# Reordering the products of the first pair, its loads and the staging sums of a gated feed-forward kernel

## The chip, the cores and the metric

The kernel runs on one NeuronCore of a Trainium2 chip. The metric is the device time of one execution, in microseconds (us). Each comparison was run on one chip with the kernel before beside it. All executions told of here were classed as fast ones. With a single core there is no second core to compare with, so a run counts as slow only where it is over 1.5% above the fastest of its kernel. Where a "slow execution" is spoken of below, one of about 542 us or more inside that class is meant.

Ratios are computed as the mean time of one kernel's fast runs over the mean of the other's fast runs of the same rounds, with a 95% interval. They are not quite the ratio of the medians that stand beside them.

## The reference

```python
B, S, D, F = 1, 2048, 1024, 3584           # all bfloat16
def reference(x, w_gate, w_up, w_down):
    return (gelu(x @ w_gate) * (x @ w_up)) @ w_down   # tanh approximation
```

## The kernel before

x is handled in two halves of 1024 rows (`h`), each as two column blocks of 512 (`xT[0]`, `xT[1]`, transposed, so that the contraction lies on the partitions). The 28 blocks of 128 columns of w_gate and w_up are taken two at a time: a **pair**. For a pair and for each of gate and up (`j`), the four products of two weight blocks with two x blocks are made with seven products instead of eight, by Strassen's method in Winograd's form. It needs sums of weight blocks (`s1` to `s4`, made by GpSimd, for the first pairs partly by VectorE) and sums of x blocks (`t1` to `t4`, made once by VectorE). The first two blocks of the first half (`first_units` and the loop over `k0`) are done in the classical way, in two halves of the contraction, since x arrives late at the start (the last of its block 1 landed at 18.50 us). The loads at the start:

```python
    for kd in range(KH, KD):
        load_xT(xT, 0, 0, kd, kd + 1)          # x block 0, second half, by DMA transposes
        if kd == KH + 1:
            for j in range(2):
                load_w(first, j, 5, KD, act, 0, FA)   # rows 5..7 of w_gate, w_up, columns 0..255
    for j in range(2):
        load_w(first, j, 0, KD, sp, FA, FG)    # columns 256..511, all rows, 512 KB each
    for k0 in range(0, KD, KH):
        load_xT(xT, 0, 1, k0, k0 + KH)         # x block 1 in two halves
```

`act` and `sp` are the queues of ScalarE and SyncE, `KD` is 8 and `KH` is 4. Every operation goes through a helper that keeps the program order of its engine. `banks` are the eight PSUM banks, the buffers in which TensorE's products are collected; a bank has to be emptied before the next product goes there. `m5` is one of the seven products, which VectorE adds to others. One pair:

```python
        def m2():
            for j in range(2):
                mm(P_[j], j, block(key, j, 0, 1), b21, False)
                if j == 0:
                    g[0] = gelu(banks[P_[0]], nxt is None)
                else:
                    mult(hT, g[0], banks[P_[1]], f0, 0)       # VectorE, frees the PSUM bank
        ...
        if part != 1:
            for j in range(2):
                mm(P_[j], j, block(key, j, 0, 0), b11, True)  # product 1
                act(nc.scalar.copy(out=banks[QB[j]][:], in_=banks[P_[j]][:]))
        if part == 0:
            m2()
            return
        behind = len(pending) > 0
        if behind:
            pending.pop()()                                   # product 2 of the pair before
        done("m2 of last")                                    # hook: work for other engines
        ...
        for j in range(2):
            add_m5(QB[j], QB[j])                              # L412: VectorE adds m5 in PSUM
            prep(j, "s2")
        ...
```

and the order of the first pair:

```python
            first_units(hT)
            first_pair = PPG - 1                   # pair 1
            for j in range(2):
                s_sum(0, first_pair, j, "s1")
                s_sum(0, first_pair, j, "s3")
            s_sum(0, first_pair, 0, "s2", True)    # True: on VectorE
            s_sum(0, first_pair, 0, "s4", True)
            t_sum("t1")
            pair_quads(hT, 0, first_pair, (0, PPG), {}, 0)    # products 1 and 2
            ...
            t_sum("t2")
            for k0 in range(0, KD, KH):            # both classical halves
                ...
```

The second projection, by w_down, uses sums of w_down's blocks too. They are **staged** during the pairs of the first half: `stage_load(i)` brings two blocks of w_down, `stage_step(n)` makes one of three sums of them on VectorE (the first and the third into a new buffer, named `o_sb`, the second in place) and stores two of them to memory. There are 4 staging sums per pair. `stage_x` transposes columns of the next x in the same way, its first eight into place and its last eight into an `o_sb` buffer, from which `store_x` stores them. There are four `o_sb` buffers for both.

```python
    def stage_step(n):
        i, k = n // 3, n % 3
        w = staged[i][0]
        if k != 1:
            staged[i].append(o_pool.tile([P, DN], F32R, name="o_sb")[:])
        t = staged[i][-1]
        in0, in1 = (lambda: (w[:, 0, DN:D], w[:, 0, 0:DN]), ...)[k]()   # (cut)
        dve(nc.vector.tensor_tensor(out=t, in0=in0, in1=in1, op=ALU.subtract))
        if k > 0:
            sp(nc.sync.dma_start(out=t_dram[:, k - 1, i, :], in_=t.bitcast(F32)))
    ...
            if h == 0 and pair >= PPG:             # from pair 2 on
                n = [min(4 * (pair - PPG + d), NSTEP) for d in range(3)]
                steps = [lambda k=k: stage_step(k) for k in range(n[0], n[1])]
                new = range((n[1] + 2) // 3, (n[2] + 2) // 3)
                then["m2 of last"] = (
                    then.get("m2 of last", [])     # in even pairs: load 2 MB of weights
                    + steps[:2]                    # two sums at the pair's start ("early")
                    + [lambda q=q: stage_x(*q) for q in xs[:2]]
                )
                then["m7"] = [store_x] + [lambda i=i: stage_load(i) for i in new]
                then["m4"] = steps[2:]             # two at its end ("late")
                xs = xs[2:]
```

## Time and profile before

| | before |
|---|---|
| time, median of 3 runs | 541.68 us (541.52 to 541.92) |
| span of the profiled execution | 539.7 us |
| TensorE (PE) busy | 534.5 us, 99% |
| VectorE (DVE), ScalarE (ACT), GpSimd (POOL) busy | 67%, 49%, 44% |

One place it did not read is VectorE's timeline at the end of pair 2, 45 us. Columns: start, duration, engine, line, operation, output and inputs, shape, count, and in brackets the idle time with its releaser.

```profile
45.73 0.68 DVE L599 TENSOR_TENSOR o_sb<-wd_sb,o_sb 128x512 fp32r<-128x512 bf16 x1
46.33 1.64 DVE L599 TENSOR_TENSOR o_sb<-wd_sb 128x512 fp32r<-128x512 bf16 x1
```

L599 is the staging sum (L605 in the changed kernel). Where it doesn't have to wait for GpSimd it takes 0.68 us; 1.64 is what one takes that starts inside a GpSimd sum (here one from 45.79 to 47.43). The reader is to keep these two sizes in mind.

### The profile page before, as it was taken

Reading aid. Unit: us, or ns where it says so; the run is one execution under the profiler, and the core shown is the slowest. Engines: PE = TensorE matmul, PEld = TensorE weight load, DVE = VectorE, ACT = ScalarE, POOL = GpSimd, SP = SyncE. Lnnn points to the kernel's source line nnn. Section 1 sums busy time; section 2 is a strip of 40 time slices with the busy share of each in tenths; the row PEclk is TensorE's granted clock in tenths of the full one; section 3 lists DMA queues with packets and bytes.
Section 4 is the critical chain, followed back from the end, with each engine's and each line's share of the span. In section 5 each row is a group of like instructions: output and inputs, shape, how many; then the busy total and the mean of one; then the engine's idle time right before and its main releaser. Section 6 shows DMA issues by size and latency. Waiting matters only on the chain.

```text
span 539.7 us, 7117 instructions
## 1 busy us (share of the span) xinstructions
PE 534.5 (99%) x2384; PEld 377.1 (70%) x2384; DVE 362.2 (67%) x475; ACT 263.3 (49%) x446; POOL 239.5 (44%) x210
## 2 busy tenths in 40 slices
PE   8999999999999999999999999999999999999997
PEld 3577777666776676767776677777777766866865
DVE  0978777787875997889574434444444469969951
ACT  1555555555555319216465555555555551452270
POOL 1369877777776000000056776666777730000000
PEclk9999999999999999999999999999999999999999
DMA  9927687695827876789950404041331466677846
GB/s 231 310 84 215 203 247 227 198 274 185 286 77 252 296 244 223 257 265 314 319 187 1 156 1 157 9 147 55 102 110 48 157 199 218 229 242 242 288 147 209
DMA packets 84772, 102.70 MB, mean 190 GB/s; under 512 B 18688, under 2 KB 66304, under 8 KB 84736
## 3 DMA queue, kind: packets, MB, share of 16 engines
q1 hardware_dynamic: 61936, 80.30, 46.2%
q10 hardware_dynamic: 22800, 21.96, 13.2%
q8 instruction: 19, 0.31, 0.2%
q14 instruction: 17, 0.14, 0.1%
HBM read 85.98 MB, written 12.58 MB: 183 GB/s over the span
## 4 chain that ended last, share of the span: by engine, by line
PE 93%; SPq 2%; DVE 1%; issue 1%; DMA 1%; ACT 0%; ACTq 0%; DVEq 0%
PE bank L389 61%; PE bank L664 33%; SPq L172 2%; DMA xT<-in_x_dram 1%; SPq L161 0%; DVE hT L277 0%; DVE t_mem L245 0%; DVE bank L412 0%; DVE s_mem L358 0%; DVE t_mem L239 0%; ACT o_sb L717 0%; SPq L167 0%; ACTq L717 0%; DVEq L239 0%
## 5 line engine op out<-in xcount | busy, mean ns | idle before, releaser
L389 PE MATMUL bank<-t_mem,s_mem 128*128 128x512 f32 x1056 | 249.7, 394 | 0.2 <-DVE bank L412 0.2
L389 PEld LDWEIGHTS bank<-t_mem,s_mem 128*128 128x128 f32 x1056 | 198.2, 188 | 44.3 <-DVE bank L412 0.9
L360 POOL TENSOR_TENSOR s_mem<-w_mem 128x512 fp32r<-128x512 bf16 x104 | 121.9, 1195 | 196.8 <-DVE t_mem L245 116.2
L277 DVE TENSOR_TENSOR hT<-w_mem,bank 128x512 bf16<-128x512 f32 x104 | 71.2, 686 | 86.6 <-PE bank L389 46.2
L664 PE MATMUL bank<-t_mem,s_mem 128*128 128x512 f32 x544 | 127.2, 392 | 0.0
L664 PEld LDWEIGHTS bank<-t_mem,s_mem 128*128 128x128 f32 x544 | 102.1, 188 | 22.2
L412 DVE TENSOR_TENSOR bank<-bank,m 128x512 f32<-128x512 f32 x108 | 69.8, 693 | 44.9 <-ACT m L434 42.7
L389 PE MATMUL bank<-xT,w_mem 128*128 128x512 bf16 x432 | 98.1, 380 | 0.2 <-DMA w_mem<-in_w_up_dram 0.2
L272 ACT ACTIVATE w_mem<-bank 128x512 f32<-128x512 f32 x104 | 61.8, 596 | 54.0 <-DVE bank L412 36.3
L389 PEld LDWEIGHTS <-w_mem 128*128 128x128 bf16 x432 | 40.1, 98 | 52.1 <-issue 6.8
L574 DVE TENSOR_TENSOR t_mem<-w_mem 128x1024 fp32r<-128x1024 bf16 x56 | 65.6, 1217 | 0.0
L360 POOL TENSOR_TENSOR s_mem<-w_mem,s_mem 128x512 fp32r<-128x512 bf16 x50 | 62.2, 1268 | 0.0
L360 POOL TENSOR_TENSOR s_mem<-s_mem,w_mem 128x512 fp32r<-128x512 f32 x50 | 58.0, 1180 | 0.0
L439 ACT COPY bank<-bank 128x512 f32<-128x512 f32 x54 | 30.8, 570 | 39.0 <-PE bank L389 38.5
L373 ACT CAST s_mem<-w_mem 128x512 fp32r<-128x512 bf16 x54 | 33.0, 615 | 30.5 <-PE bank L389 29.2
L639 DVE TENSOR_TENSOR s_mem<-hT 128x512 fp32r<-128x512 bf16 x52 | 34.2, 685 | 10.2 <-PE bank L664 9.4
L434 ACT COPY m<-bank 128x512 f32<-128x512 f32 x54 | 31.7, 587 | 18.4 <-PE bank L389 18.3
L664 PEld LDWEIGHTS <-hT 128*128 128x128 bf16 x224 | 21.2, 98 | 26.7 <-issue 2.1
L444 ACT COPY bank<-bank 128x512 f32<-128x512 f32 x54 | 30.8, 570 | 12.8 <-PE bank L389 12.8
L717 ACT CAST o_sb<-bank 128x512 bf16<-128x512 f32 x28 | 15.3, 585 | 39.6 <-PE bank L664 39.6
L599 DVE TENSOR_TENSOR o_sb<-wd_sb,o_sb 128x512 fp32r<-128x512 bf16 x28 | 31.4, 1121 | 0.5
L571 ACT CAST t_mem<-w_mem 128x1024 fp32r<-128x1024 bf16 x28 | 26.9, 1047 | 0.0
(44 smaller groups left out, 235.7 us busy)
## 6 DMA issues: line engine op xcount, KB each, us to landing
t_mem<-t_dram SPq DMA_DIRECT2D x56, 512.0 KB, 5.4
w_mem<-in_w_gate_dram ACTq DMA_DIRECT2D x10, 1024.0 KB, 5.6
w_mem<-in_w_up_dram ACTq DMA_DIRECT2D x10, 1024.0 KB, 8.7
wd_sb<-in_w_down_dram SPq DMA_DIRECT2D x28, 256.0 KB, 5.0
t_dram<-o_sb SPq DMA_DIRECT2D x28, 256.0 KB, 2.4
wd_sb<-in_w_down_dram SPq DMA_DIRECT2D x12, 512.0 KB, 8.4
w_mem<-in_w_down_dram SPq DMA_DIRECT2D x10, 512.0 KB, 5.8
w_mem<-in_w_down_dram SPq DMA_DIRECT2D x4, 1024.0 KB, 6.3
```

Source lines behind the costliest of these rows:

```text
L272: act(nc.scalar.activation(out=g_sb, in_=ps[:], func=ACT.Gelu_apprx_tanh))
L277: nc.vector.tensor_tensor(out=hT[:, fc, tb * TB : (tb + 1) * TB], in0=g_sb, in1=ps[:], op=ALU.mult,)
L360: pool(nc.gpsimd.tensor_tensor(out=t, in0=in0, in1=in1, op=op))
L373: act(nc.scalar.copy(out=t, in_=a(1, 1)))
L389: nc.tensor.matmul(banks[bank][:], lhsT=lhs[:, c, :], rhs=rhs[:, c, :], start=start and c == 0, stop=c == KH - 1, skip_group_check=True,)
L412: nc.vector.tensor_tensor(out=banks[dst][:], in0=banks[src][:], in1=m5[j][:], op=ALU.add)
L434: act(nc.scalar.copy(out=m5[j][:], in_=banks[V_[j]][:]))
L439: act(nc.scalar.copy(out=banks[RB[j]][:], in_=banks[QB[j]][:]))
L574: dve(nc.vector.tensor_tensor(out=t, in0=in0, in1=in1, op=ALU.subtract))
L599: dve(nc.vector.tensor_tensor(out=t, in0=in0, in1=in1, op=ALU.subtract))
L639: dve(nc.vector.tensor_tensor(out=t, in0=in0, in1=in1, op=op))
L664: nc.tensor.matmul(banks[bset[u]][:], lhsT=lhs(i, u), rhs=rhs(i), start=start and i == 0, stop=stop and i == NS - 1, skip_group_check=True,)
```

## The change

Its intent: w_up's last rows take the other queue, so that ScalarE is not blocked; columns 256 to 511 and x's block 1 arrive in halves, each half of the weights ahead of the half of x that needs it; and the first pair follows that order: product 1, the first classical half, product 2 (`part` 2), the second classical half, the rest. VectorE's sums follow, s1 among them, which GpSimd made before; its multiply of product 2 (`out11`) is deferred, and the second half of t4 is split into two quarters between the additions of m5. Last, the staging sums run two steps late, so that pair 2 starts without any.

```diff
--- before.py
+++ after.py
@@ -208,10 +208,10 @@
         load_xT(xT, 0, 0, kd, kd + 1)
         if kd == KH + 1:
             for j in range(2):
-                load_w(first, j, 5, KD, act, 0, FA)
-    for j in range(2):
-        load_w(first, j, 0, KD, sp, FA, FG)
+                load_w(first, j, 5, KD, (act, sp)[j], 0, FA)
     for k0 in range(0, KD, KH):
+        for j in range(2):
+            load_w(first, j, k0, k0 + KH, sp, FA, FG)
         load_xT(xT, 0, 1, k0, k0 + KH)
     new_chunk((0, 1))
     for j in range(2):
@@ -425,8 +425,11 @@
                 mm(P_[j], j, block(key, j, 0, 1), b21, False)
                 if j == 0:
                     g[0] = gelu(banks[P_[0]], nxt is None)
-                else:
-                    mult(hT, g[0], banks[P_[1]], f0, 0)
+                elif part != 2:
+                    out11()
+
+        def out11():
+            mult(hT, g[0], banks[P_[1]], f0, 0)
 
         def do_m5(j):
             mm(V_[j], j, s(j, "s1"), tsum["t1"], True)
@@ -438,13 +441,14 @@
             mm(QB[j], j, s(j, "s2"), tsum["t2"], False)
             act(nc.scalar.copy(out=banks[RB[j]][:], in_=banks[QB[j]][:]))
 
-        if part != 1:
+        if part not in (1, 2):
             for j in range(2):
                 mm(P_[j], j, block(key, j, 0, 0), b11, True)
                 act(nc.scalar.copy(out=banks[QB[j]][:], in_=banks[P_[j]][:]))
-        if part == 0:
+        if part == 2:
             m2()
-            return
+        if part in (0, 2):
+            return out11
         behind = len(pending) > 0
         if behind:
 
@@ -467,11 +471,13 @@
                 done("m6")
         for j in range(2):
             add_m5(QB[j], QB[j])
+            done(f"q{j}")
             prep(j, "s2")
         done("m5")
         for j in range(2):
             mm(RB[j], j, s(j, "s3"), tsum["t3"], False)
             add_m5(V_[j], RB[j])
+            done(f"v{j}")
             prep(j, "s3")
             if j == 0:
                 g[1] = gelu(banks[V_[0]], nxt is None)
@@ -817,18 +823,15 @@
             first_units(hT)
             first_pair = PPG - 1
 
+            nxt = (0, PPG)
             for j in range(2):
-                s_sum(0, first_pair, j, "s1")
                 s_sum(0, first_pair, j, "s3")
-            s_sum(0, first_pair, 0, "s2", True)
-            s_sum(0, first_pair, 0, "s4", True)
+            pair_quads(hT, 0, first_pair, nxt, {}, 0)
             t_sum("t1")
-            pair_quads(hT, 0, first_pair, (0, PPG), {}, 0)
             for j in range(2):
                 s_sum(0, first_pair, j, "a22")
-            t_sum("b22")
-            s_sum(0, first_pair, 1, "s2", True)
-            t_sum("t2")
+                for name in ("s1", "s2"):
+                    s_sum(0, first_pair, j, name, True)
             for k0 in range(0, KD, KH):
                 for u, bset in enumerate((PB, RB)):
                     for b, w_sb in zip(bset, chunks[first]):
@@ -838,12 +841,16 @@
                         unit_out(hT, bset, u, 1)
                     if k0 > 0 and u == 0:
                         t_sum("t3")
+                if k0 == 0:
+                    out11 = pair_quads(hT, 0, first_pair, nxt, {}, 2)
+                    t_sum("b22")
+                    t_sum("t2")
+                    s_sum(0, first_pair, 0, "s4", True)
+            t_sum("t4", 0, KH // 2)
             s_sum(0, first_pair, 1, "s4", True)
-            t_sum("t4", 0, KH // 2)
             xs = [(tb, kd) for tb in (1, 0) for kd in range(KD)]
             new_x(1)
             stage_load(0)
-            stage_load(1)
         for pair in range(first_pair, NPAIR):
             then = {}
             if pair % PPG == 0 and (pair // PPG + 1) * PPG < NPAIR:
@@ -858,17 +865,20 @@
                     then["m2 of last"] = [load_chunk]
             if h == 0 and pair >= PPG:
 
-                n = [min(4 * (pair - PPG + d), NSTEP) for d in range(3)]
+                n = [
+                    min(max(4 * (pair - PPG + d) - 2, 0), NSTEP) for d in range(3)
+                ]
                 steps = [lambda k=k: stage_step(k) for k in range(n[0], n[1])]
+                early_steps = steps[: len(steps) - 2]
                 new = range((n[1] + 2) // 3, (n[2] + 2) // 3)
 
                 then["m2 of last"] = (
                     then.get("m2 of last", [])
-                    + steps[:2]
+                    + early_steps
                     + [lambda q=q: stage_x(*q) for q in xs[:2]]
                 )
                 then["m7"] = [store_x] + [lambda i=i: stage_load(i) for i in new]
-                then["m4"] = steps[2:]
+                then["m4"] = steps[len(early_steps) :]
                 xs = xs[2:]
             if pair == NPAIR - 2:
 
@@ -912,8 +922,8 @@
                 }
             if pair < PPG and h == 0:
 
-                def late_t4():
-                    t_sum("t4", KH // 2, KH)
+                def late_t4(c):
+                    t_sum("t4", c, c + 1)
                     last_on["t4"] = last_on["dve"]
 
                 def late_s():
@@ -922,7 +932,12 @@
                         for j in range(2):
                             s_sum(0, PPG, j, name)
 
-                then = {"m5": [late_t4], "m4": [late_s]}
+                then = {
+                    "q0": [lambda: late_t4(KH - 2)],
+                    "v0": [lambda: late_t4(KH - 1)],
+                    "v1": [out11],
+                    "m4": [late_s],
+                }
             nxt = (h, pair + 1) if pair + 1 < NPAIR else None
             part = 1 if (h, pair) == (0, PPG - 1) else None
             pair_quads(hT, h, pair, nxt, then, part)
```

## The prediction

> **What bounds the kernel now.** I read the page's table of engines first: TensorE (PE) is busy 534.5 of 539.7 us, while VectorE (DVE) has 67%, ScalarE 49%, GpSimd 44%. Part 4 of the page, the chain that ended last, is 93% PE. So only idle time or lost pitch of PE can be won, and a busy share does not show lost pitch, since one matmul's record (380 to 394 ns) is longer than the distance between two. I therefore read the timeline of PE over the first 50 us and divided distances between starts by counts. Columns: start, duration from first start to last end, engine, line, operation, tiles, shape, count, and in brackets the idle time with its releaser.
>
> ```profile
> 6.68 4.30 PE L253 MATMUL bank<-xT,w_mem 128*128 128x512 bf16 x18
> 11.13 2.33 PE L253 MATMUL bank<-xT,w_mem 128*128 128x512 bf16 x10 [0.15 <-DMA w_mem<-in_w_up_dram]
> 13.30 1.03 PE L389 MATMUL bank<-xT,w_mem 128*128 128x512 bf16 x4
> 14.54 2.76 PE L389 MATMUL bank<-xT,w_mem 128*128 128x512 bf16 x12 [0.21 <-DMA w_mem<-in_w_up_dram]
> 17.14 7.07 PE L253 MATMUL bank<-xT,w_mem 128*128 128x512 bf16 x32
> 23.86 7.78 PE L389 MATMUL bank<-t_mem,s_mem 128*128 128x512 f32 x32
> 31.85 2.10 PE L389 MATMUL bank<-t_mem,s_mem 128*128 128x512 f32 x8 [0.21 <-DVE bank L412]
> 33.80 1.90 PE L389 MATMUL bank<-xT,w_mem 128*128 128x512 bf16 x8
> 35.35 9.44 PE L389 MATMUL bank<-t_mem,s_mem 128*128 128x512 f32 x40
> 44.63 3.63 PE L389 MATMUL bank<-xT,w_mem 128*128 128x512 bf16 x16
> 47.91 2.42 PE L389 MATMUL bank<-t_mem,s_mem 128*128 128x512 f32 x9
> ```
>
> The steady part: from 14.54 to 17.14 twelve bf16 matmuls take 2.60 us, 0.216 each. From 35.35 to 47.91, 12.56 us, lie 40 f32 and 16 bf16 matmuls; less 16 x 0.216 = 3.46 that leaves 0.227 per f32 one. Later pairs repeat the same 12.56 us, so nothing is to be won after 33.8 us. Up to there: 6.68 to 11.13 is 4.45 us for 18 matmuls (3.89 needed): **0.56 lost**. 13.30 to 14.54 is 1.24 for 4 (0.86): **0.37 lost**. 17.14 to 31.85 is 14.71 for 32 bf16 and 32 f32 (6.91 + 7.26 = 14.17): **0.5 lost** (single starts put 0.11 at 29.5 and 0.37 just before 31.85). 31.85 to 33.80 is 1.95 for 8 (1.82): **0.1 lost**. In sum 1.5 us, all that this change can reach.
>
> What causes each: the ScalarE timeline tells of part of the first, the DVE timeline of the last two.
>
> ```profile
> 4.49 0.38 ACTq L161 DMA_DIRECT2D w_mem<-in_w_gate_dram  x1
> 7.46 0.47 ACTq L161 DMA_DIRECT2D w_mem<-in_w_up_dram  x1
> 8.03 0.58 ACT L314 COPY xT<-bank 128x512 bf16<-128x512 bf16 x1 [4.36 <-DMA w_mem<-in_w_gate_dram]
> ...
> ```
>
> ```profile
> 14.69 0.91 DVE L358 TENSOR_TENSOR s_mem<-s_mem,w_mem 128x512 fp32r<-128x512 f32 x1
> 15.63 1.52 DVE L358 TENSOR_TENSOR s_mem<-w_mem,s_mem 128x512 fp32r<-128x512 bf16 x1
> 17.07 3.24 DVE L236 TENSOR_TENSOR t_mem<-xT,xT 128x2048 fp32r<-128x2048 bf16 x1
> ...
> 28.78 1.28 DVE L412 TENSOR_TENSOR bank<-bank,m 128x512 f32<-128x512 f32 x2
> 29.98 1.21 DVE L245 TENSOR_TENSOR t_mem<-xT,t_mem 128x1024 fp32r<-128x1024 bf16 x1
> 31.11 1.28 DVE L412 TENSOR_TENSOR bank<-bank,m 128x512 f32<-128x512 f32 x2
> ```
>
> The tail of w_up (rows 5 to 7) is issued by ScalarE only at 7.46: its issue waits for an earlier load's semaphore, whose load landed at 7.44. ScalarE's copy of x block 3 stands behind it and ends at 8.61; PE's next weight load starts at 8.66, 0.25 us late. The same load lands at 11.09 and PE resumes at 11.13, 0.31 late. In the DVE timeline the engine has no gap from 14.69 to 32.4; the reader is to see that PE's third and fourth losses end on L412, the additions of m5, and that a 1.21 us half of t4 stands between the two pairs of them.
>
> **What the Trainium skill says.** "TensorE: Matmul & The Clock Gate", section "Wait — 56ns, not 53.3ns?", gives 215.7 ns between starts of warm 512-column matmuls; this trace agrees with 216 for bf16, and has 227 for the fp32r ones. "VectorE: DVE Perf Modes", "The perf-mode tier table", gives 2293 ns for an fp32 tensor_tensor of 2048 elements; t2 and t3 took 2.28 us here. "SBUF — State Buffer", "Who interferes with whom": a DVE instruction with two SBUF inputs contends with a GpSimd instruction that reads SBUF. The trace agrees: sums that take 0.68 us alone took 0.91 and 1.52, and t1 3.24 instead of 2.28, while GpSimd ran its four sums (12.78 to 18.16). "DMA: Bandwidth & Descriptors", "Issuing engines are not separate DMA queues": issuing from another engine saves only sequencer time. That fits a load whose harm was to block ScalarE's sequencer.
>
> **The change, part by part.** No matmul is added or removed; only the order and waits of the first 34 us change.
>
> 1. *w_up's tail moves from ScalarE's queue to SP's, between transposes.* SP can issue it about 4.9, or 5.7 at worst if it must await x's second load (landed 5.65), so it lands near 9.5 (estimate: 4.6 us from issue to landing for the 192 KB w_up load before it). PE wants it at 10.6. The copy no longer waits. Gain 0.25 + 0.31 = 0.56. Price: transposes of blocks 6 and 7 land some 0.6 us after their 9.47 and 9.95; PE wants them at 11.0 and 11.9, so hidden.
> 2. *Columns 256 to 511 load in k-halves.* Before, the two 512 KB loads landed at 12.71 and 14.49, and PE stopped until 14.54. Now both first halves together are 512 KB, so the second of them lands about when the first load did, 12.7. First units end at 13.30 - 0.56 = 12.74; product 1's second half wants it at 13.6. Gain 0.37.
> 3. *The classical half takes product 2's place.* It starts at 12.74 + 8 x 0.216 = 14.47 and needs the first half of transposed x, which landed at 16.51. With 512 KB less ahead of it, at the 1.8 to 2.0 us per 512 KB that the neighbouring landings show, it lands at 14.5 to 14.8. **New wait: 0.1 to 0.4.** Product 2 (from about 18.2) wants second halves at perhaps 16.7; the second classical half (from about 20.0) wants the other x half at 18.5 as before. Both hidden.
> 4. *DVE's order.* t1 starts at about 14.8 instead of 17.07, and GpSimd has only two sums left (s3), done by about 14.1, so t1 takes 2.28: done 17.1 instead of 20.3. It pays with two more s1 sums (2 x 0.60). By my walk in program order: four s-sums to 19.5, t2 to 21.8, s4 to 22.4, multiply 23.2, t3 25.5, multiply 26.1, half of t4 27.2, s4 27.8. Then the m5 additions and two t4 quarters of 0.6 interleave: additions done near 28.4, 29.6, 30.2, 31.4. PE, at about 23.4 when m5 starts, wants them at about 28.9, 29.8, 30.7, 31.6. All met, some by only 0.2. Gain 0.6 less about 0.1.
> 5. *Two staging sums leave the start of pair 2, the deferred multiply (0.65) enters.* DVE is freed of 2 x 0.7 to 0.8 where GpSimd makes pair 2's sums. Those were in time already (f32 block from 35.35 without a stall), so no gain on the path. Two sums appear later in pair 12, where DVE has a gap of 2.6 us: free.
>
> Sum: 0.56 + 0.37 + 0.6 = 1.5, less 0.25 for x's half and 0.1 for tight additions: 1.15 to 1.2 us. 541.68 - 1.2 = **540.5 us**.
>
> **Rivals.** (a) *x's first half becomes the new wait in full.* The transfer row shows those transposes slow (SP spent 5.40 us issuing the first); if they don't come earlier with fewer bytes ahead, PE waits from 14.5 to 16.5, and the kernel gets 0.5 to 1 us slower: about 542.4. Against it: the DMA engines are at their limit there (share about 1.1), so bytes, not issue, set the landing. (b) *DVE stays the bound.* Its work between 14.7 and 32 is nearly all there; if t1 gets no earlier start or the sums run beside GpSimd, items 1 to 3 are eaten by a wait on L412, and only 0.2 to 0.5 us remain: 541.3. For it: 17 us without a gap. Against: 1.0 us of t1's time was contention, and 2.3 us its late start. (c) *Everything hides*: all 1.5 gone, 540.1.
>
> **Range and chances.** The 2% mark is 10.8 us, seven times what is lost in the whole region, so faster by it is ruled out and slower would need a stall of a kind that nothing here suggests. Repeats of before spread 0.4 us. Range 539.9 to 541.3: low is (c) with spread, high is (b).
>
> **What would show it.** PE timeline of after: no gap on w_up near 11 or 14; 18 + 10 matmuls in about 6.05 us; a short wait on x's transpose near 14.5; no wait on L412; first pair over near 32.6 instead of 33.8; 12.56 us per pair afterwards. DVE: t1 in 2.28 us from about 14.8. The prediction is wrong if PE waits over 0.6 us for x's halves, if additions still end PE's waits, or if a later pair loses its pitch through the shifted staging sums.

## More of the kernel before

The page follows the chain of work that ended last back from the end; this is its share by engine:

```profile
PE 93%; SPq 2%; DVE 1%; issue 1%; DMA 1%; ACT 0%; ACTq 0%; DVEq 0%
```

Nearly everything that is not PE in it lies in the first 34 us. The prediction reads that region.

## The result, and the profile after

| | before, same rounds | after |
|---|---|---|
| median of 6 runs | 541.59 us | 542.61 us |
| lowest to highest | 541.22 to 541.92 | 540.65 to 544.28 |
| ratio of fast runs | | 1.0018 [0.9998, 1.0038] |

542.61 lies 1.3 us above the predicted range. The six times were 540.65, 542.7, 544.28, 542.36, 542.61 and 542.6. **The profile was taken of the first, which is the only one within the range.** So the profile after shows the kernel at its best, and nothing in it can show where the other five lost 2 us. Its chain:

```profile
PE 98%; DMA 1%; ACT 0%; issue 0%; DVE 0%; ACTq 0%
```

PE's timeline of the start, in the columns as before:

```profile
6.61 6.39 PE L253 MATMUL bank<-xT,w_mem 128*128 128x512 bf16 x28
12.84 1.89 PE L389 MATMUL bank<-xT,w_mem 128*128 128x512 bf16 x8
14.59 3.63 PE L253 MATMUL bank<-xT,w_mem 128*128 128x512 bf16 x16
18.05 1.89 PE L389 MATMUL bank<-xT,w_mem 128*128 128x512 bf16 x8
19.78 3.62 PE L253 MATMUL bank<-xT,w_mem 128*128 128x512 bf16 x16
23.04 9.46 PE L389 MATMUL bank<-t_mem,s_mem 128*128 128x512 f32 x40
32.35 1.90 PE L389 MATMUL bank<-xT,w_mem 128*128 128x512 bf16 x8
33.90 9.44 PE L389 MATMUL bank<-t_mem,s_mem 128*128 128x512 f32 x40
```

No line has a releaser. Product 1 (12.84), classical half (14.59), product 2 (18.05), half (19.78) and the forty fp32 matmuls follow one another at full pitch; 33.80 of before has become 32.35. VectorE's timeline, t1 and the end of pair 2:

```profile
14.63 2.29 DVE L236 TENSOR_TENSOR t_mem<-xT,xT 128x2048 fp32r<-128x2048 bf16 x1 [0.33 <-DMA xT<-in_x_dram]
...
44.28 1.58 DVE L605 TENSOR_TENSOR o_sb<-wd_sb 128x512 fp32r<-128x512 bf16 x1
45.89 1.53 DVE L605 TENSOR_TENSOR o_sb<-wd_sb,o_sb 128x512 fp32r<-128x512 bf16 x1
```

t1 takes 2.29 us instead of 3.24, as predicted. The two staging sums at 44.28 and 45.89 take one contended length each, and after them all is in time. From 33.90 on the pairs keep 12.56 us.

### The profile page after: what moved, and what is told of

Same layout as the page of the kernel before. It is cut to its first block, busy times and chain, and to the rows that moved or that the text cites. A ratio compares the mean times of both kernels' runs of the same rounds, so it can differ in the third digit from the quotient of the medians.

```text
span 538.9 us, 7121 instructions
## 1 busy us (share of the span) xinstructions
PE 533.7 (99%) x2384; PEld 377.3 (70%) x2384; DVE 363.8 (68%) x478; ACT 263.1 (49%) x446; POOL 236.5 (44%) x208
## 4 chain that ended last, share of the span: by engine, by line
PE 98%; DMA 1%; ACT 0%; issue 0%; DVE 0%; ACTq 0%
PE bank L389 63%; PE bank L670 33%; PE bank L253 3%; DMA w_mem<-in_x_dram 1%; PE bank L304 0%; ACT o_sb L723 0%; DVE xT L312 0%; ACTq L723 0%
## 5 line engine op out<-in xcount | busy, mean ns | idle before, releaser
L360 POOL TENSOR_TENSOR s_mem<-w_mem 128x512 fp32r<-128x512 bf16 x102 | 118.5, 1183 | 198.5 <-DMA w_mem<-in_w_up_dram 102.4
L277 DVE TENSOR_TENSOR hT<-w_mem,bank 128x512 bf16<-128x512 f32 x104 | 71.0, 686 | 82.9 <-PE bank L389 43.1
L412 DVE TENSOR_TENSOR bank<-bank,m 128x512 f32<-128x512 f32 x108 | 69.8, 694 | 46.5 <-ACT m L437 42.5
```

The costliest lines, as they stand in the source:

```text
L277: nc.vector.tensor_tensor(out=hT[:, fc, tb * TB : (tb + 1) * TB], in0=g_sb, in1=ps[:], op=ALU.mult,)
L360: pool(nc.gpsimd.tensor_tensor(out=t, in0=in0, in1=in1, op=op))
L412: nc.vector.tensor_tensor(out=banks[dst][:], in0=banks[src][:], in1=m5[j][:], op=ALU.add)
```

## The experiments

**Theory.** The reordered start gives its 1.2 us in all executions, and something later takes 2 us in most of them. The part of the change that reaches past 34 us is the staging schedule, so it is the first suspect. **Rival 1:** the slow executions lose the time at the start, where loads land a little differently each time. **Rival 2:** the six runs were a poor sample. Eighteen runs were made; the runs of one call shared a chip and the runs of the kernel before. This table has them all; the last column tells what TensorE lost after 34 us in the execution that was profiled (distance of two starts less the usual 0.227 us, if over 0.2 us in one place; in brackets what the first pair lost).

| run | median us (range), runs | before | ratio [95%] | profiled us: lost after 34 us |
|---|---|---|---|---|
| after_again | 543.06 (541.99 to 543.97), 6 | 541.67 | 1.0026 [1.0013, 1.004] | 541.99: 1.2 at 49, 0.3 at 128 |
| order_only | 540.8 (540.43 to 541.13), 5 | 541.67 | 0.9986 [0.9974, 0.9998] | 540.74: none |
| stage_only | 542.93 (542.01 to 544.74), 6 | 541.67 | 1.0029 [1.0015, 1.0043] | 542.93: 0.5 at 50, 0.9 at 54 |
| loads_only | 545.42 (545.24 to 546.1), 5 | 541.67 | 1.0075 [1.0062, 1.0087] | (start: 1.5, 1.5, 0.3, 0.6, 0.4) |
| moved_sums | 542.96 (542.45 to 544.25), 6 | 541.55 | 1.0023 [0.9994, 1.0051] | 542.82: 1.8 at 52 |
| early_sums | 541.32 (540.85 to 542.8), 6 | 541.55 | 0.9992 [0.9964, 1.0021] | 541.11: none |
| gpsimd_sums | 544.76 (543.75 to 545.6), 6 | 541.55 | 1.0046 [1.0015, 1.0077] | 545.6: 3.0 at 52, half clock after, 0.4 at 107 |
| old_loads | 542.3 (542.18 to 542.7), 4 | 541.55 | 1.0007 [0.9973, 1.004] | (start: 0.3, 0.4, 1.2) |
| after_third | 542.63 (542.43 to 542.78), 6 | 541.52 | 1.0015 [1.0003, 1.0028] | 542.7: 1.2 at 50, 0.2 at 104 |
| no_vector_sums | 540.87 (540.44 to 542.84), 6 | 541.52 | 0.9991 [0.9973, 1.0008] | 542.84: 1.6 at 102, 0.7 at 466 |
| late_start | 543.11 (542.11 to 546.43), 6 | 541.52 | 1.0035 [1.001, 1.006] | 546.43: 2.7 at 104, half clock after |
| order_again | 540.64 (540.35 to 542.81), 6 | 541.52 | 0.9987 [0.9969, 1.0005] | 540.52: none |
| loads_first | 542.37 (541.75 to 543.47), 6 | 541.38 | 1.0016 [1.0002, 1.0029] | 542.49: 1.2 at 49, 0.3 at 104 |
| neither | 540.99 (540.41 to 545.11), 6 | 541.38 | 0.9998 [0.9974, 1.0023] | 540.53: none |
| late_loads_first | 542.35 (541.9 to 542.75), 6 | 541.38 | 1.0015 [1.0002, 1.0028] | 542.11: 1.6 at 102 |
| order_loads_first | 540.57 (540.49 to 541.86), 6 | 541.38 | 0.9985 [0.9973, 0.9998] | 540.99: none |
| late_skip_x | 540.88 (540.85 to 541.46), 5 | 541.45 | 0.999 [0.9978, 1.0003] | 540.88: none |
| neither_skip_x | 540.28 (540.03 to 540.9), 5 | 541.45 | 0.9975 [0.9961, 0.9989] | 540.9: 0.6 at 464 |

The gaps under 0.2 us are not told in the table; order_only has three of about 0.1 us between 39.8 and 40.9 us, a point to which the end returns.

### First call: the parts by themselves

**after_again** is the changed kernel once more, without an edit.

> The changed kernel once more, unaltered. Its first measurement gave 540.65 in the execution that was profiled (span 538.9) and 542.4 to 544.3 in the other five, so the profile may show the one good execution. Theory A (the slow executions are a lasting property of the changed kernel): the median of the timed executions is again 542 to 543 and a profile, if it falls in one, shows an added PE stall of about 2 us in one or more places. Theory B (a chance of that chip): the median is 540.3 to 540.8.

It took 543.06. This time the profiled execution was one that lost time.

**order_only** is the changed kernel with the former staging schedule:

```diff
             stage_load(0)
+            stage_load(1)
...
-                n = [min(max(4 * (pair - PPG + d) - 2, 0), NSTEP) for d in range(3)]
+                n = [min(4 * (pair - PPG + d), NSTEP) for d in range(3)]
-                early_steps = steps[: len(steps) - 2]
+                early_steps = steps[:2]
```

> The changed kernel with the staging schedule of the kernel before (two staging loads early, four sums in pair 2, two early and two late sums per pair). Theory A1 (the shifted staging schedule makes VectorE wait for weight-down loads that land with 0.1 us to spare, and that stalls PE in some executions): 540.3 to 540.7 in every execution, spread under 0.5. Theory A2 (the new tight waits for x and the k-halves at the start make the slow executions): stays at 542 to 543 with a spread of 2 or more.

**stage_only** is the reverse, the kernel before with the new staging schedule only:

> The kernel before with the staging schedule of the changed one alone. Theory A1 (staging causes the slow executions): 543 to 544 with a spread of 1.5 or more. Theory A2 (the start does): 541.5 as the kernel before, spread 0.5.

order_only took 540.8, 2.3 us less than the whole change on the same chip, and stage_only 542.93, 1.3 us more than before. So the schedule costs 1.3 us with the former start and 2.3 with the new one. This ends rival 2, since the median of the unedited change came out slow again, and most of rival 1, since no execution of order_only, with the new start, took over 541.13, and none of stage_only, with the former one, under 542.01. Some tenths do vary at the start: in the profiles of the new start and loads PE loses 0 to 0.6 us on x's half at 14.5.

**loads_only** is the kernel before with the loads alone changed (the first hunk of the diff):

> The kernel before with the load part of the change alone (tail of w_up on SP's queue, columns 256 to 511 in k-halves), products and sums in the old order. By my prediction's items 1 and 2 it gains at the start 0.56 + 0.37, less what the late DVE chain takes back: PE has no gap on w_up, but the waits on the m5 additions grow. 540.8 to 541.5. Theory A2 (loads at the start cause slow executions): 542 or more in some of its executions.

It took 545.42, where 540.8 to 541.5 was expected. Two lines of PE's timeline say why:

```profile
16.24 1.90 PE L389 MATMUL bank<-xT,w_mem 128*128 128x512 bf16 x8 [1.34 <-DMA w_mem<-in_w_gate_dram]
...
27.33 5.30 PE L389 MATMUL bank<-t_mem,s_mem 128*128 128x512 f32 x20 [1.36 <-DVE t_mem L239]
```

Product 2 straight behind product 1 wants the second halves of the weights, which now land later, and t2 comes late with them. The loads by themselves make the start slower by 3.8 us: they are of use only with the order that follows them.

### The first cause: a sum that is passed over

The slow execution, told from the run after_third (the changed kernel on a third chip, again without an edit; after_again and loads_first show the same picture):

> The changed kernel a third time, for one more profile and five more times on the chip of the runs beside it. Lock-out theory: if the profiled execution takes over 541.5, its trace shows the first late staging sum of pair 2 at over 3 us and a PE wait behind it near 49 us; if it takes under 541, that sum takes under 1.8 us. A slow profile without it would refute the theory.

VectorE's timeline at the end of pair 2:

```profile
44.89 4.95 DVE L605 TENSOR_TENSOR o_sb<-wd_sb 128x512 fp32r<-128x512 bf16 x1
49.87 0.69 DVE L605 TENSOR_TENSOR o_sb<-wd_sb,o_sb 128x512 fp32r<-128x512 bf16 x1
50.48 0.68 DVE L277 TENSOR_TENSOR hT<-w_mem,bank 128x512 bf16<-128x512 f32 x1
```

GpSimd's timeline in the same execution:

```profile
44.77 2.26 POOL L360 TENSOR_TENSOR s_mem<-w_mem 128x512 fp32r<-128x512 bf16 x2
46.98 2.30 POOL L360 TENSOR_TENSOR s_mem<-w_mem,s_mem 128x512 fp32r<-128x512 bf16 x2
50.24 1.33 POOL L360 TENSOR_TENSOR s_mem<-w_mem 128x512 fp32r<-128x512 bf16 x1 [0.96 <-PE bank L389]
```

and PE's:

```profile
51.21 3.02 PE L389 MATMUL bank<-t_mem,s_mem 128*128 128x512 f32 x12 [1.05 <-DVE hT L277]
```

The reader is to see three things. The sum at 44.89 is recorded as one instruction of 4.95 us, against 1.58 in the fast execution and 0.68 alone. Through it GpSimd makes four sums, 44.77 to 49.28, at the length that they have when nobody is beside them (some 1.15 us each); the VectorE sum ends 0.56 us after the last of them, so it did its work when GpSimd paused. (The expectations call this a lock-out.) And the multiply behind it in program order (L277, 50.48) is what empties a PSUM bank for TensorE, which waits 1.05 us for it. The staging sum itself is wanted by nobody soon: it cost time only because the multiply stands behind it in VectorE's program order.

In stage_only the same sum took 4.24 us, in after_again 4.94 and in loads_first 4.94. All four profiles of slow executions with this schedule have it, and the one fast profile (540.65) has 1.58.

With the former schedule the same place looks like this, in VectorE's timeline of order_again (the changed start with the former schedule, run a second time):

```profile
44.63 1.03 DVE L605 TENSOR_TENSOR o_sb<-wd_sb,o_sb 128x512 fp32r<-128x512 bf16 x1
45.59 1.64 DVE L605 TENSOR_TENSOR o_sb<-wd_sb 128x512 fp32r<-128x512 bf16 x1
```

and in GpSimd's:

```profile
45.07 3.19 POOL L360 TENSOR_TENSOR s_mem<-w_mem 128x512 fp32r<-128x512 bf16 x2
```

There are two sums in the same place, but here the two engines take turns: the VectorE sums take 1.03 and 1.64 us, and GpSimd's are stretched to 1.6. Which of the sums comes first is different, and so is its arrival (neither is shown to be the reason, see "Open"): in order_again 0.68 us into a GpSimd sum with fp32 input (43.95 to 45.11), in after_third 0.12 us into one of two bf16 inputs.

> The changed order of products and loads with the old staging schedule again, beside the others on one chip. Expected 540.5 to 541.1, 0.6 to 1.0 under the kernel before, as in its first run (540.8 against 541.67).

order_again took 540.64: the result of order_only holds on a second chip, though one of its six runs took 542.81.

The second call tried to move the two late sums of pair 2 away. **moved_sums** makes them at the start of pair 3, four there in all:

```diff
-                steps = [lambda k=k: stage_step(k) for k in range(n[0], n[1])]
-                early_steps = steps[: len(steps) - 2]
+                lo = 0 if pair == PPG + 1 else n[0]
+                hi = lo if pair == PPG else n[1]
+                steps = [lambda k=k: stage_step(k) for k in range(lo, hi)]
+                early_steps = steps[: max(len(steps) - 2, 0)]
```

> The changed kernel, its two late staging sums of pair 2 moved behind the next multiply, to the start of pair 3 (four sums there, two late; later pairs as in the changed kernel). Lock-out theory (in the slow executions the first late sum of pair 2 waits out four GpSimd sums, 4.2 to 4.9 us instead of 0.68, and the multiply that frees a PSUM bank stands behind it, so PE waits 0.5 to 1.2 us, twice in some executions): 540.3 to 541.0, spread under 1. Rival, phase theory (the shift of the staging steps in pairs 3 to 12, whose loads land with 0.1 us to spare, is what costs): stays at 542 to 544.

No sum took over 1.75 us, so the lock-out was gone, and yet it took 542.96: four sums in a row (1.72, 0.69, 1.54, 1.65 us) stood ahead of the additions of m5, and PE waited 1.6 us for L412. A place was removed and a new one made.

**early_sums** makes the two at the start of pair 2 and none at its end (`early_steps = steps[: 2 if pair == PPG else len(steps) - 2]`):

> The changed kernel, its two staging sums of pair 2 put at the pair's start, where the kernel before has two of its four, and none at its end. Lock-out theory: the sums then run beside GpSimd at 33 to 35 us, as in the kernel before and in the run with the old staging schedule, where each waited for one GpSimd sum at most; 540.4 to 541.1. Phase theory: 542 to 544. If any first sum in GpSimd's long run can be locked out, wherever it stands: 541.5 or more, with a spread over 1.5.

541.32, with no long sum and nothing over 0.2 us lost after 34 us in the profiled run (541.11). The ratio's interval spans 1, so this alone doesn't prove much; two of its six runs, 542.17 and 542.8, are slow.

**gpsimd_sums** gives the two late sums to GpSimd, so that they can't contend with it:

```diff
-        dve(nc.vector.tensor_tensor(out=t, in0=in0, in1=in1, op=ALU.subtract))
+        if on_pool:                                    # the two late ones of pair 2
+            pool(nc.gpsimd.tensor_tensor(out=t, in0=in0, in1=in1, op=ALU.subtract))
+        else:
+            dve(nc.vector.tensor_tensor(out=t, in0=in0, in1=in1, op=ALU.subtract))
```

> The changed kernel, its two late staging sums of pair 2 made by GpSimd itself behind its own sums[...]. Lock-out theory: no VectorE sum over 1.8 us anywhere, no PE wait near 49 us; 540.3 to 540.8 with a spread under 0.8. Phase theory: 542 to 544. A third possibility, GpSimd too late with the sums for pair 4 because of 2.4 us more work: PE waits in pair 4.

It was the slowest but one, 544.76, and as a test it failed: the next VectorE sum needs the second of them, waited 3.5 us for it, and the additions behind it were late. PE waited 2.79 us for L412, and then ran at half its clock for 3.4 us (a window view of 56.4 to 59.8 us shows a granted clock of 0.50).

**old_loads** asks the opposite of loads_only: order_only with the loads of the kernel before.

> The run with the changed products and the old staging schedule (540.8), with the loads of the kernel before put back. By items 1 to 3 of my prediction the w_up gaps come back (0.56 + 0.37) and x's first transposed half lands at about 16.5 while PE wants it at about 15.3, so PE waits another 1 us or so there: 542 to 543. Rival: the order of products alone carries the gain and the loads matter little: 541.

542.3, which is 1.5 us more than order_only's 540.8 on another chip (before took 541.55 and 541.67 there): PE lost 0.3 us at 8.1, 0.4 at 13.7 and 1.2 at 15.0, the last on the first half of x's block 1. So the new order needs the new loads as well.

**no_vector_sums** is the test of the first cause. It gives a wrong result (relative error 0.376): the two late sums of pair 2 become copies made by ScalarE, everything else stays.

```diff
-        dve(nc.vector.tensor_tensor(out=t, in0=in0, in1=in1, op=ALU.subtract))
+        if n < 2:
+            act(nc.scalar.copy(out=t, in_=in0))
+        else:
+            dve(nc.vector.tensor_tensor(out=t, in0=in0, in1=in1, op=ALU.subtract))
```

> The changed kernel with the two late staging sums of pair 2 replaced by ScalarE copies of the first operand (a wrong result on purpose: one block of the staged sums is false). Nothing else moves[...]. Lock-out theory: 540.2 to 540.9 with a spread under 1. Phase theory (the shifted loads of later pairs): stays at 542 to 544.

540.87 against 542.63 for the unedited change on the same chip: four of its six runs lie at 540.44 to 540.97, where all six of the unedited change lie at 542.43 or more. So these two sums are what the median lost; that they lose it by waiting behind GpSimd is read from the traces. But single runs stayed slow (542.84 and 541.98), and the profile happened to be of one of them: PE loses 1.6 us at 102 us. There is a second cause.

### The second cause: sums that wait for x's late transposes

**late_start** was meant to be the correct kernel without the first cause: no staging sum in pair 2, four or five in each later pair.

```diff
-                n = [min(max(4 * (pair - PPG + d) - 2, 0), NSTEP) for d in range(3)]
+                n = [sum((0, 4, 4, 5, 5, 4, 4, 4, 4, 4, 4)[: pair - PPG + d]) for d in range(3)]
-                early_steps = steps[: len(steps) - 2]
+                early_steps = steps[:2]
```

> The changed kernel with no staging sum in pair 2 at all: 4 sums in each later pair, 5 in pairs 5 and 6, two of them early. The run with four sums moved into pair 3's start lost 1.8 us there because each sum beside GpSimd takes some 1.5 us and the m5 additions stood behind all four; here only two stand there, as in the kernel before. Lock-out theory: 540.2 to 540.8, which would be the best version. Against it: lock-outs can happen at the end of pair 3 as well, then 541.5 or more in some executions.

543.11, with a run of 546.43, which was profiled: PE waited 2.5 us for L412 at 104 us and then had half its clock for 3.4 us, a distance of 0.43 us for each of seven matmuls instead of 0.227. So its schedule makes the second place worse. That place, in VectorE's timeline of after_third:

```profile
100.39 0.69 DVE L605 TENSOR_TENSOR o_sb<-wd_sb 128x512 fp32r<-128x512 bf16 x1 [0.47 <-issue]
101.44 0.69 DVE L605 TENSOR_TENSOR o_sb<-wd_sb,o_sb 128x512 fp32r<-128x512 bf16 x1 [0.36 <-DMA wd_sb<-in_w_down_dram]
```

and in the timeline of SyncE's queue (starts of issue):

```profile
88.36 6.11 SPq L619 DMA_TRANSPOSE o_sb<-in_x_dram  x2
96.48 0.80 SPq L624 DMA_DIRECT2D x_dram<-o_sb  x2
97.32 1.89 SPq L591 DMA_DIRECT2D wd_sb<-in_w_down_dram  x4
```

Both sums stand at the start of pair 7, ahead of the additions of m5, and both have waited. (The first one's 0.47 is put down to "issue"; the trace has its load landing at 100.31, 0.08 us before it starts.) The loads were issued at 97.3 and 97.8, because the queue stood behind `store_x`, which waits for two transposes. The first was issued at 88.36 and landed at 96.41, 8.1 us later, beside the 2 MB of weights that pair 6 loads (issued from 85.7, landed by 96.45); in pair 7, which loads none, the same took 3.6 and 3.1 us. The second shares a row with it in the view but was issued only at 93.35, and landed at 96.73: the queue had waited 3.6 us for the store of a staged sum out of an `o_sb` buffer, which took 6.5 us beside the same weights. The shift by two steps is why it matters here: pair 7 now starts with steps 18 and 19, the first two of a new load, where before it started with 20 and 21, of which only the second needs the new load.

**loads_first** issues the staging loads ahead of the store, in the changed kernel:

```diff
-                then["m7"] = [store_x] + [lambda i=i: stage_load(i) for i in new]
+                then["m7"] = [lambda i=i: stage_load(i) for i in new] + [store_x]
```

> The changed kernel with one line more: on the SyncE queue, the staging loads of each pair are issued ahead of the store of x instead of behind it. The changed kernel's profiled executions show two places where TensorE is held: 48.9 to 49.8 us (the first staging sum of pair 2, locked out behind GpSimd for 4.9 us; 1.2 us lost) and about 102 to 104 us (pair 7: its first staging sums wait for a load that is issued late because the queue stands behind the store of x; 0.2 to 1.6 us). Theory of two causes: the second place goes, the lock-out stays: 542.2 to 542.8, no run of 543.5 or more. If the lock-out were the only cause: spread as before, 541.99 to 544. If the load were the main cause: 540.3 to 541.0.

542.37. The first load now landed at 97.03, 3.5 us before the sum started, and the sum waited all the same, even longer, in VectorE's timeline:

```profile
100.55 0.69 DVE L605 TENSOR_TENSOR o_sb<-wd_sb 128x512 fp32r<-128x512 bf16 x1 [0.96 <-issue]
```

The expectation that the load was the wait was therefore wrong, although the time lies in the expected range of 542.2 to 542.8. The trace has the store of x landing at 100.47, 0.08 us before this start: the sum needs a new `o_sb` buffer, and x's columns hold it until they are stored. Under the late load lay a second wait for the same late transposes.

**neither** is no_vector_sums with the same line, **late_loads_first** is late_start with it, **order_loads_first** order_only with it.

> Wrong on purpose: the changed kernel with pair 2's two late staging sums turned into ScalarE copies (no VectorE sum stands in GpSimd's run of sums) and with the staging loads ahead of the store of x. Both suspected causes are away. Theory of two causes: 540.2 to 540.8 in every fast run and no TensorE distance over 700 ns after 40 us. If a third cause is at work: the median stays over 541 or single runs of 542 to 544 stay.

> The changed kernel with no staging sum in pair 2 at all, four or five in each later pair, and the staging loads ahead of the store of x. Its earlier version without that last part took 543.11, with a stall of 2.5 us at 104 us where VectorE's staging sums waited for landings (101.3 and 103.1 us). Theory of two causes: with the loads earlier it takes 540.2 to 540.8. If the packing of four or five sums per pair itself delays the m5 additions: 541.5 or more with the stall still in place.

> The changed kernel with the former schedule of staging sums (540.8 and 540.64 in two earlier runs) and the staging loads ahead of the store of x. Neither cause is present without the last part in the profiled executions, so it should change nothing: 540.4 to 540.9. If the store of x, which now comes later, matters: over 541.

neither: 540.99 (540.2 to 540.8 was expected of every run), five runs of 540.41 to 541.19 and one of 545.11. late_loads_first: 542.35, with 1.6 us lost at 102; its sum at 99.23 waited 0.7 us, in that trace named outright as for the store of x. So the edit did not take the second cause away. order_loads_first: 540.57, nothing lost by the edit.

The last call removes what the two waits share. **late_skip_x** (from late_start) and **neither_skip_x** (from no_vector_sums, wrong by 0.376 as that one) stage no x into `o_sb` buffers in the pairs that load weights (6, 8 and 10):

```diff
+                loads_w = pair % PPG == 0 and (pair // PPG + 1) * PPG < NPAIR
+                take = 0 if loads_w and xs and xs[0][0] == 0 else 2
-                    + [lambda q=q: stage_x(*q) for q in xs[:2]]
+                    + [lambda q=q: stage_x(*q) for q in xs[:take]]
-                xs = xs[2:]
+                xs = xs[take:]
```

> The changed kernel with no staging sum in pair 2 (four or five in each later pair), and without the staging of x's second half in those pairs that load a chunk of weights (pairs 6 and 8; it runs two pairs longer instead). In the run that issued the staging loads first, the sum at 99 to 100 us no longer waited for its load but for a buffer that x's transposed columns held until they were stored; those transposes land 8 us late because they stand behind the chunk of weights. Theory (two causes, the second being x's late transposes, through loads and buffers alike): no lock-out, no wait of a sum at 99 to 103 us, no TensorE distance over 700 ns after 40 us, 540.2 to 540.8. If four or five sums per pair delay the m5 additions by themselves: the stall at 102 us stays and it takes 541.8 or more.

> Wrong on purpose: the changed kernel's own schedule, with the two late sums of pair 2 turned into ScalarE copies, and without the staging of x's second half in the pairs that load a chunk of weights. It took 540.87 and 540.99 with one cause less treated, with single runs of 542 to 545. Theory of two causes: 540.3 to 540.8, the sum at 99 us without a wait, and no more single runs over 541.5 than the kernel before has. If single runs of 542 to 545 stay as frequent, they come from something else.

late_skip_x took 540.88 (540.85 to 541.46), 2.2 us less than the 543.11 of late_start against nearly the same time of before. The sum in its VectorE timeline has no wait any more:

```profile
99.11 0.68 DVE L605 TENSOR_TENSOR o_sb<-wd_sb 128x512 fp32r<-128x512 bf16 x1
```

neither_skip_x, the changed kernel with both causes taken away, took 540.28, five runs from 540.03 to 540.9, ratio 0.9975 [0.9961, 0.9989]. That is 1.2 us under before, the gain that was predicted, and no run of 542 or more is left. The former schedule with this edit was not run, so it stays open how much of the 1.2 us comes from staging x elsewhere and not from undoing the harm of the shift. In five runs a rare slow one can be missed, though: before itself had single runs of 546.42 and 543.34, with which no experiment here deals.

## Why the prediction was right or wrong

1. *w_up's tail*: right. 28 matmuls take 6.23 us, 12.84 less 6.61, of which 0.17 are one longer distance at 7.26; 6.05 was predicted. The load was issued at 4.85 and landed at 9.66 (4.9 and 9.5 predicted).
2. *Halves of columns 256 to 511*: right. They landed at 11.83 and 12.72 (12.7 predicted), and product 1 runs through.
3. *x's half as a new wait of 0.1 to 0.4*: right as to place, and nearly as to size. It landed at 14.54 and cost nothing in the profiled run, 0.3 us in after_third, 0.5 in late_skip_x, 0.6 in order_loads_first. Rival (a) did not come true: a longer wait there, 1.2 us, shows only with the former loads, in old_loads. That the measured 542.61 lies beside the 542.4 of rival (a) is chance.
4. *VectorE's order*: right. t1 at 14.63 took 2.29, PE never waits on L412, and the first pair is over at 32.35, for which 32.6 was predicted. Rival (b) fell.
5. *The staging shift*: **this step failed.** The prediction said of the two sums that leave "so no gain on the path", and of the two that appear later, "free", since VectorE has a gap of 2.6 us in pair 12. The shift by itself cost 1.3 us (stage_only, 542.93 against 541.67). The prediction looked at the two ends of the shift only. All sums between them move too: another sum stands at the end of pair 2, with another arrival against GpSimd's sums, and pairs between start with the first sums of a new load instead of its last. The first cost 1.2 us in three of the four profiles of slow executions and 1.4 in stage_only (0.5 and 0.9), late loads like those of the second 0.2 to 0.3 us in three of those four (at 104 us, or at 128 in after_again), and the second up to 1.6 us in no_vector_sums. The medians of the change and of the former schedule lie 2.0 to 2.3 us apart (543.06 and 540.8, 542.63 and 540.64), and the profiles account for a part of that: of the 2.2 us between after_third and order_again, 1.0 was lost in pairs 2 and 3 (net of the gain of 0.3 told below), 0.3 at 104 us, 0.6 before 34 us and 0.3 after 440. The last sentence of the prediction names this risk, but its range gave it no room: 541.3 was the high end of rival (b).

"No gain on the path" was wrong by a little as well: order_only, order_again and early_sums have three distances 0.1 us too long between 39.5 and 41 us. They have staging sums at the start of pair 2 behind the new start; the changed kernel, with none there, doesn't show them. So the shift gains 0.3 us in that place and loses more in others.

What the whole sum was worth is indicated by the changed kernel freed of both causes: 540.28, against 540.5 predicted. It is no proof of the sum, since that kernel also makes two sums less on VectorE and stages x in other pairs. **The version to keep is order_only or order_loads_first**, the new start with the former staging schedule: three results of 540.57 to 540.8, ratios 0.9985 to 0.9987, two of the three intervals wholly under 1, with single runs of 542.81 and 541.86. late_skip_x, at 0.999 [0.9978, 1.0003], is no better.

**Open:** why the sum is passed over at this place and the engines take turns elsewhere. The arrival relative to GpSimd's sum doesn't tell it: 0.12 us after a GpSimd sum's start in the fast execution (44.28 against 44.16) and 0.12 in after_third (44.89 against 44.77). GpSimd's timeline in the fast execution, to be laid beside that of after_third, where the same two sums took 2.26 us:

```profile
44.16 2.72 POOL L360 TENSOR_TENSOR s_mem<-w_mem 128x512 fp32r<-128x512 bf16 x2
```

Open too is what the slowest executions of the change lost: those of 543.7 to 544.3 were timed but not profiled. The second cause (1.6 us in no_vector_sums, 2.7 in late_start) is a candidate.

## What to carry to other kernels

When a change shifts a schedule, look at every place through which it shifts, above all at the one instruction that now stands ahead of a multiply or an addition that frees a PSUM bank; where an engine's program order is kept, a sum that nobody needs soon can hold up one that TensorE needs now. When a profile is faster than the median of its runs, it is a profile of the wrong execution: run the kernel again until a slow one is caught. And when a wait is removed and another of the same size takes its place, look for what both have in common; here the late staging of x held both a queue and a buffer.

## What the Trainium skill lacked or had wrong

- "SBUF — State Buffer", section "Who interferes with whom", says that a VectorE instruction with two SBUF inputs contends with a GpSimd instruction that reads SBUF, and, of the two-port modes, that whoever issues first has the shared ports for the whole instruction while the other fully blocks; issue order, it adds, decides who blocks. It doesn't say who comes next when several GpSimd instructions follow one another. The runs show both: taking turns (VectorE 1.5 to 1.6 us instead of 0.68, GpSimd 1.6 instead of 1.15), and a VectorE sum passed over for three or four GpSimd sums in a row (4.24, 4.94, 4.94 and 4.95 us), of which all but the first started after it, so issue order alone doesn't tell.
- "TensorE: Matmul & The Clock Gate", section "Why this matters for your kernels", advises against idle gaps over about 3 us between bursts of matmuls. Here waits of 2.5 us (late_start) and 2.79 us (gpsimd_sums) were followed by 3.4 us at a granted clock of 0.50, while waits of 1.0 to 1.6 us were not.
- On none of the pages did I find a figure for the distance of 512-column matmuls with fp32r operands (227 ns here), or for how long a DMA transpose takes while a bulk load runs: here 8.1 us from issue to landing beside 2 MB of weights, and 3.1 and 3.6 without them (after_third).
